# Attention accumulations of a decode kernel with gradients: four cache blocks per matmul, 512 wide

## The chip, the cores and the metric

The kernel runs on one core of a Trainium2 chip. Time is device time in microseconds (us), from the first to the last instruction as the chip reports it. The kernel before the change takes 1138.2 us, the median of three runs (1136.74 to 1139.24).

## The reference

Two identical decoder layers, one token for each of two sequences, forward and backward. A layer is grouped attention over a long cache and then a small MLP; both layers use the same caches and the same weights. Cut to what matters here:

```python
B, Sq, D = 2, 1, 1024
Hq, Hkv, Sk, Dh = 32, 4, 16384, 128          # 8 query heads share one cache head

def _A_ref(x, k_cache, v_cache, wq, wo):
    q = (x @ wq).reshape(B, Sq, Hq, Dh).transpose(0, 2, 1, 3)
    k, v = repeat(k_cache, 8, axis=1), repeat(v_cache, 8, axis=1)
    scores = einsum("bhqd,bhkd->bhqk", q, k) * (Dh ** -0.5)
    p = softmax(scores)
    o = einsum("bhqk,bhkd->bhqd", p, v)
    return o.transpose(0, 2, 1, 3).reshape(B, Sq, Hq * Dh) @ wo

x = x + _A_ref(_layernorm(x), k_cache, v_cache, wq, wo)     # layer 0
x = x + _B_ref(_layernorm(x), w1, b1, w2, b2)
x = x + _A_ref(_layernorm(x), k_cache, v_cache, wq, wo)     # layer 1
x = x + _B_ref(_layernorm(x), w1, b1, w2, b2)
# returned: x and the gradients of all inputs, for a given grad_out
```

There are 2 x 4 = 8 groups g (a sequence and a cache head), each with a K and a V cache of 16384 x 128 in bf16, 4 MB. Four sums over a whole cache concern us: the forward output o = sum of p x V in layer 0 and in layer 1, and in the backward pass of each layer dq = sum of ds x K, where ds is the gradient of the scores.

## The kernel before

A cache of 16384 rows is kept as 128 partitions x 128 blocks: partition p holds rows 128p to 128p + 127, and "block t" is row t of every partition, a matrix of 128 x 128. The kernel reads a cache in four chunks of 32 blocks, 1 MB each, into a ring of seven buffers. The exponentials of both layers stay in e_all, for group, pair of blocks u, layer l, head h and block t within the pair:

```python
TC = 32; NCH = T // TC; CP = TC // 2; NP = T // 2       # T = 128 blocks
e_all = pers.tile([128, G, NP, 2, 8, 2], BF16, name="e_all")
ACCT = pa([128, 512], F32, "acc_all")                   # one PSUM bank
```

One call of `quad` adds 16 blocks to an accumulator. The stationary operand of a matmul is the 16 columns of coefficients of one pair (8 heads x 2 blocks), the moving operand is two blocks of the cache side by side, 256 wide. Four of these matmuls go to four groups of 32 columns of the array (and 32 partitions of the accumulator), and four more follow. Of each 16 x 256 result only the parts where the block of the coefficient is that of the cache are wanted; sel2 picks these, and adds the four partition groups and the two blocks, in `reduce`:

```python
sel2 = const.tile([128, 16], F32, name="sel2")          # four 16-wide pieces of the identity, added
sel2v = sel2[:].rearrange("p (h t) -> p t h", t=2)

class Acc:
    def __init__(self, g, src, coef, finish, half=0):
        self.acc = ACCT[:, half * 256:half * 256 + 256] if half < 2 else pm_([128, 256], F32, "acc2")[:]
        zero = lambda: V.memset(self.acc, 0.0)
        ...

    def quad(self, c, q, coef=None):
        ...
        for i in range(8):
            u = c * CP + q * 8 + i
            cg = 32 * (i % 4)
            t = 2 * (q * 8 + i)
            PE.matmul(self.acc[cg:cg + 16, :], lhsT=coef(u),
                      rhs=self.cv[:, t:t + 2, :].rearrange("p t d -> p (t d)"),
                      start=False, stop=True, tile_position=(0, cg), skip_group_check=True)      # L452

    def evac(self):
        self.sb = wrk.tile([128, 2, 128], F32, name="acc_sb")
        evac_cast(self.sb[:].rearrange("p a b -> p (a b)"), self.acc, 256)
        ...

    def reduce(self):
        ps = px([128, 8], F32, "o_ps")[:] if self.alloc is None else self.alloc()[:, 0:8]
        for t in range(2):
            PE.matmul(ps, lhsT=self.sb[:, t, :], rhs=sel2v[:, t, :], start=(t == 0), stop=(t == 1))
        self.finish(ps)
```

Two accumulators share the bank ACCT, for alternating groups. The forward pass works in slots of eight blocks: eight transposes of K blocks (L420), a copy to SBUF by ScalarE or VectorE, and two slots later eight matmuls with the queries (L573). When a group's scores are complete, 16 exponentials follow, and its eight quads on V are taken from a queue, one in two slots, while the next group's scores are made:

```python
a = Acc(g, "V", lambda u: e_all[:, g, u, l].rearrange("p h t -> p (h t)"), finish, g % 2)
...
sch.later(9, lambda: queue_acc(sch, a, range(0, 2), False))
sch.later(13, lambda: queue_acc(sch, a, range(2, 4), True))
```

The layer-1 backward pass has the same slots with V transposed (L420) and the output's gradient in place of the queries (L672). After each chunk one product on VectorE makes ds, and two quads on K follow. Two chunks' ds lie interleaved in one buffer:

```python
dXr = [wrk.tile([128, CP, 2, 8, 2], BF16, name="dX%d" % i)[:] for i in range(3)]
...
ds = dXr[k // 2 % 3][:, :, k % 2]
ev = e_all[:, g, c * CP:(c + 1) * CP, l, :, :].rearrange("p a h b -> p h a b")
V.tensor_tensor(out=ds.rearrange("p a h b -> p h a b"),
                in0=dp[:].rearrange("p h (a b) -> p h a b", b=2), in1=ev, op=ALU.mult)            # L642
...
coef = lambda u: ds[:, u - c * CP].rearrange("p h t -> p (h t)")
```

The last pass is the backward of layer 0. It also makes the gradients of both caches for both layers (L1260: four matmuls 512 wide on halves of the rows, each evacuated by a copy and stored) and those of the weights (L1174), and does layer 0's dq on the way. dX holds the ds of both layers there:

```python
accs[g].coef = lambda u: dX[i][:, u - c * CP, 0].rearrange("p h t -> p (h t)")
```

Of the kernel before, what the change touches and what calls it, by code (L numbers as in the profile page):

```python
# [10 lines left out]
F32 = mybir.dt.float32  # L11
I32 = mybir.dt.int32
ACT = mybir.ActivationFunctionType
ALU = mybir.AluOpType
# [9 lines left out]
def kernel(  # L24
# [24 lines left out]
    nc = tc.nc  # L49
# [65 lines left out]
    V.memset(ones_bf[:], 1.0)  # L115
    neghalf = const.tile([128, 2], F32, name="neghalf")
    V.memset(neghalf[:], -0.5)
    sel2 = const.tile([128, 16], F32, name="sel2")
    V.tensor_tensor(out=sel2[:], in0=identf[:, 0:16], in1=identf[:, 32:48], op=ALU.add)
    V.tensor_tensor(out=sel2[:], in0=sel2[:], in1=identf[:, 64:80], op=ALU.add)  # L120
    V.tensor_tensor(out=sel2[:], in0=sel2[:], in1=identf[:, 96:112], op=ALU.add)
    sel2v = sel2[:].rearrange("p (h t) -> p t h", t=2)
    e_all = pers.tile([128, G, NP, 2, 8, 2], BF16, name="e_all")
    hot3 = const.tile([128, 128], BF16, name="hot3")
    m3 = const.tile([128, 1], F32, name="m3")
    V.tensor_reduce(out=m3[:], in_=identf[:, 64:128:32], axis=AX.X, op=ALU.add)
# [298 lines left out]
    class Acc:  # L425

        def __init__(self, g, src, coef, finish, half=0):
            self.g, self.src, self.coef, self.finish = g, src, coef, finish  # L430
            self.pre = {}
            self.cv = None
            self.acc = ACCT[:, half * 256:half * 256 + 256] if half < 2 else pm_([128, 256], F32, "acc2")[:]
            self.half = half
            zero = lambda: V.memset(self.acc, 0.0)
            if half in Acc.in_use:
                Acc.then[half] = zero
            else:
                zero()
            Acc.in_use.add(half)  # L440

        def quad(self, c, q, coef=None):
            coef = coef or self.coef
            if q == 0 and self.get is not None:
                self.cv = self.get(c)
            elif q == 0:
                self.cv = self.pre.pop(c) if c in self.pre else kv_load(self.src, self.g, c)
            for i in range(8):
                u = c * CP + q * 8 + i
                cg = 32 * (i % 4)  # L450
                t = 2 * (q * 8 + i)
                PE.matmul(self.acc[cg:cg + 16, :], lhsT=coef(u),  # L452
                          rhs=self.cv[:, t:t + 2, :].rearrange("p t d -> p (t d)"),
                          start=False, stop=True, tile_position=(0, cg), skip_group_check=True)

        def evac(self):
            self.sb = wrk.tile([128, 2, 128], F32, name="acc_sb")
            evac_cast(self.sb[:].rearrange("p a b -> p (a b)"), self.acc, 256)
            if self.half in Acc.then:
                Acc.then.pop(self.half)()  # L460
            else:
                Acc.in_use.remove(self.half)

        def reduce(self):
            ps = px([128, 8], F32, "o_ps")[:] if self.alloc is None else self.alloc()[:, 0:8]
            for t in range(2):
                PE.matmul(ps, lhsT=self.sb[:, t, :], rhs=sel2v[:, t, :], start=(t == 0), stop=(t == 1))
            self.finish(ps)

        alloc = get = None  # L470
# [30 lines left out]
    def attn_fwd(l, q_bf, rbc, oT, groups):  # L501
        sch = Sched()
        slots = [(g, c, b) for g in groups for c in range(NCH) for b in range(NB)]
        kTs, sc, st = {}, {}, {}

        def max_half(g, f):
            m = small.tile([128, 8], F32, name="mx%d" % f)
            V.tensor_reduce(out=m[:], in_=sc[g][f][:], axis=AX.X, op=ALU.max)
            charge("D", 0.7)
            st[g].append(m)  # L510

        def post(g):
            max_half(g, 1)
            m0, m1 = st[g]
            V.tensor_tensor(out=m0[:], in0=m0[:], in1=m1[:], op=ALU.max)
            esum = small.tile([128, 2, 8], F32, name="esum")
            negm = small.tile([128, 8], F32, name="negm")
            box = {}

            def p1():  # L520
                box["pm"] = pm_([8, 128], F32, "pm")
                PE.transpose(box["pm"][:, :], m0[:], identf[:])
                gm = small.tile([8, 1], F32, name="gm")
                V.reduce_max(out=gm[:], in_=box["pm"][:, :], axis=AX.X)
                box["dg"] = small.tile([8, 8], F32, name="dg")
                V.tensor_scalar(out=box["dg"][:], in0=identf[0:8, 0:8], scalar1=gm[:, 0:1], scalar2=None, op0=ALU.mult)
                charge("D", 0.5)

            def p2():
                pm2 = pm_([128, 8], F32, "pm2")  # L530
                PE.matmul(pm2[:], lhsT=onesf[0:8, :], rhs=box["dg"][:], start=True, stop=True)
                V.tensor_scalar(out=negm[:], in0=pm2[:], scalar1=-1.0, scalar2=None, op0=ALU.mult)  # L532
                charge("D", 0.2)

            def ex(f, h):
                half = NP // 2
                S.activation(out=e_all[:, g, f * half:(f + 1) * half, l, h, :],  # L537
                             in_=sc[g][f][:, h, :].rearrange("p (a b) -> p a b", b=2),
                             func=ACT.Exp, bias=negm[:, h:h + 1], scale=1.0, accum_out=esum[:, f, h:h + 1])
                charge("A", 0.3)  # L540

            def fin1():
                V.tensor_tensor(out=esum[:, 0, :], in0=esum[:, 0, :], in1=esum[:, 1, :], op=ALU.add)

            def fin2():
                pm3 = part_sum(esum[:, 0, :], 8, "pm3")
                V.reciprocal(out=rbc[:, g, :], in_=pm3[:])

            def finish(ps):
                V.tensor_tensor(out=oT[:, g, :], in0=ps, in1=rbc[:, g, :], op=ALU.mult)  # L550

            a = Acc(g, "V", lambda u: e_all[:, g, u, l].rearrange("p h t -> p (h t)"), finish, g % 2)
            sch.later(2, p1)
            sch.later(4, p2)
            for i in range(16):
                sch.later(5 + i // 2, lambda i=i: ex(i // 8, i % 8))
            sch.later(9, lambda: queue_acc(sch, a, range(0, 2), False))
            sch.later(13, lambda: queue_acc(sch, a, range(2, 4), True))
            sch.later(14, fin1)
            sch.later(15, fin2)  # L560

        def score(s):
            g, c, b = slots[s]
            if c == 0 and b == 0:
                sc[g] = {}
                st[g] = []
            kT = kTs.pop(s)
            for j in range(8):
                t = c * TC + b * 8 + j
                f = t // TH  # L570
                if t % TH == 0:
                    sc[g][f] = px([128, 8, TH], F32, "sc")
                PE.matmul(sc[g][f][:, :, t % TH], lhsT=kT[:, j, :], rhs=q_bf[:, g, :], start=True, stop=True)  # L573
            if c == NCH // 2 - 1 and b == NB - 1:
                max_half(g, 0)
            if c == NCH - 1 and b == NB - 1:
                post(g)

        cv = None
        s = 0  # L580
        while s < len(slots) + 2 or sch.busy():
            sch.s = s
            if s < len(slots):
                g, c, b = slots[s]
                if b == 0:
                    cv = kv_load("K", g, c)
                kTs[s] = emit_T(cv, b, True)
            sch.run_slot(1 if s < len(slots) else 2)
            if 2 <= s < len(slots) + 2:
                score(s - 2)  # L590
            s += 1

    def attn_bwd(l, do_bf, dqT, dn, groups, ahead):
# [40 lines left out]
        def post(g, c):  # L634
# [2 lines left out]
                      rhs=dlr[:, g, l, :].unsqueeze(2).to_broadcast([128, 8, TC]), start=False, stop=True)  # L637
            k = made["n"]
            made["n"] += 1
            ds = dXr[k // 2 % 3][:, :, k % 2]  # L640
            ev = e_all[:, g, c * CP:(c + 1) * CP, l, :, :].rearrange("p a h b -> p h a b")
            V.tensor_tensor(out=ds.rearrange("p a h b -> p h a b"),  # L642
                            in0=dp[:].rearrange("p h (a b) -> p h a b", b=2), in1=ev, op=ALU.mult)
# [1 line left out]
            if c == 0:  # L645
                def finish(ps, g=g):
# [4 lines left out]
                        wq_n[g % HKV][3]()  # L651
                    elif done_g.count(g % HKV) == 2:
                        by_dots(g % HKV)
                accs[g] = Acc(g, "K", None, finish, 2 if g == G - 1 else groups.index(g) % 2)
            acc = accs[g]
            if g == groups[-1]:
                accs[g].pre[c] = kv_load("K", g, c)
                if c == NCH - 1:
                    for k in range(NLD - 2):
                        ahead.load(k)  # L660
                        j0, rb = ahead.chunks[k]
                        w2_q.extend(lambda j=j: ahead.row(j) for j in range(j0, j0 + rb))
            coef = lambda u: ds[:, u - c * CP].rearrange("p h t -> p (h t)")
            sch.later(2, lambda: queue_acc(sch, acc, [c], c == NCH - 1, coef))

        def score(s):
# [658 lines left out]
    def open_dq(g):  # L1325
        def finish(ps):
            V.tensor_scalar(out=dq0[:, g, :], in0=ps, scalar1=QSCALE, scalar2=None, op0=ALU.mult)
            ready.append(g)
            if len(ready) % 2 == 0:
                quarter(g % HKV)  # L1330
        accs[g] = Acc(g, "K", None, finish, order.index(g) % 2)
        accs[g].alloc = mx
        accs[g].get = lambda c: (held_tiles["K%d" % c] if g == G - 1 else get("K", g, c))[:].rearrange(
            "p (t d) -> p t d", d=128)

    def dq_quad(i, q):
        g, c = chunks[i]
        accs[g].coef = lambda u: dX[i][:, u - c * CP, 0].rearrange("p h t -> p (h t)")
        accs[g].quad(c, q)
        if q == 1:  # L1340
            if g == G - 1:
# [202 lines left out]
```

## Time and profile before

| stage | from, us | to, us | quads in it |
|---|---|---|---|
| query projection, layer 0 | 0 | 28 | - |
| attention forward, layer 0 | 28 | 185 | 64 |
| output projection, MLP, projection of layer 1 | 185 | 271 | - |
| attention forward, layer 1 | 271 | 422 | 64 |
| MLP of layer 1, forward and backward, output projection backward | 422 | 502 | - |
| attention backward, layer 1 | 502 | 660 | 64 |
| MLP backward, layer 0, and what leads to the last pass | 660 | 737 | - |
| last pass: attention backward of layer 0, all cache and weight gradients | 737 | 1136 | 64 |

How to read the lines of the profile that follow below: PE is TensorE's matmul, PEld its weight load, DVE is VectorE, ACT ScalarE, POOL GpSimd, SP the engine that issues loads. "L452" is line 452 of the kernel. A group's line has engine, operation, output and inputs by the program's names, the active rows and columns of the array (128*16), the shape, and the count; then busy time in us and the mean duration of one in ns; then how long the engine was idle ahead of these instructions, and what it waited for. Matmuls are pipelined, so that busy time is the time covered by at least one, and the mean duration is longer than the time between two starts. In the 40 slices a digit is a share in tenths, 9 for 90% or more; PEclk is the granted share of TensorE's full clock.

The profiled execution took 1136.1 us from the first to the last instruction, with a mean granted clock of 0.882, and read 348.14 MB and wrote 98.58 MB of device memory.

### The profile page before, as it was taken

To read this page: it belongs to the slowest core of one execution; us is meant where nothing else is said; L and a number is where in the kernel's file an instruction comes from. 1 tells how busy PE (TensorE), PEld (TensorE's weight loads), DVE (VectorE), ACT (ScalarE), POOL (GpSimd) and SP (SyncE) were. 2 spreads that over 40 slices of the span, in tenths; PEclk is the share of its full clock that TensorE was granted. 3 is DMA by queue.
4 is the path that set the end of the run, shared out by engine and by line. 5 is a ranking of instruction groups with operands and counts; after the bars stand their busy time and mean duration, and the time that the engine had idled before them with its cause. 6 is when DMAs were issued, how large, how long until landed. Compare 5 with 4: busy or idle time off the path is not lost.

```text
span 1136.1 us, 38923 instructions
## 1 busy us (share of the span) xinstructions
PE 945.3 (83%) x17087; PEld 715.0 (63%) x17087; DVE 637.6 (56%) x1391; ACT 567.5 (50%) x1414; POOL 70.1 (6%) x124
## 2 busy tenths in 40 slices
PE   4978796487879885899998699988898897898896
PEld 3867675487767665898876588855555454455452
DVE  1545442133545432444746454778788767787776
ACT  0544342022535340344554344767787756686674
POOL 0000000000000000000000000022111111111210
PEclk9988976596998976899998899999999978898987
DMA  9999999998999989999999999998999999999997
GB/s 371 424 424 424 424 425 412 405 379 354 423 426 424 423 320 422 392 350 393 380 422 418 359 371 336 364 367 311 394 418 423 423 419 423 424 412 421 422 402 288
DMA packets 91962, 449.24 MB, mean 395 GB/s; under 512 B 7302, under 2 KB 7302, under 8 KB 54672
## 3 DMA queue, kind: packets, MB, share of 16 engines
q1 hardware_dynamic: 74448, 354.46, 77.4%
q0 software_dynamic: 17344, 92.29, 19.7%
q8 instruction: 133, 2.18, 0.7%
q14 instruction: 37, 0.30, 0.1%
HBM read 348.14 MB, written 98.58 MB: 393 GB/s over the span
## 4 chain that ended last, share of the span: by engine, by line
PE 50%; DMA 31%; DVE 10%; issue 4%; ACT 3%; POOL 0%; DVEq 0%; POOLq 0%; ACTq 0%; SPq 0%
DMA kv_V<-in_A_v_cache_dram 13%; PE tp L420 10%; PE wtp L270 5%; DMA kv_K<-in_A_k_cache_dram 5%; PE tpm L1451 4%; PE acc_all L452 4%; PE xm L1260 4%; DMA wt<-in_A_wo_dram 3%; DMA out_dram<-keepK 3%; DMA keepK<-in_A_v_cache_dram 3%; PE sc L573 3%; PE turn L322 3%; PE xm L1174 3%; PE dp L1313 2%; DMA out_dram<-keepxV 2%
## 5 line engine op out<-in xcount | busy, mean ns | idle before, releaser
L153 ACT COPY kT<-tp 128x512 int32<-128x512 int32 x209 | 122.8, 587 | 256.7 <-PE tp L420 247.9
L156 DVE COPY kT<-tp 128x1024 bf16<-128x1024 bf16 x159 | 108.8, 691 | 110.0 <-PE tp L420 99.1
L420 PE MATMUL tp<-ident,kv_K 128*128 128x128 bf16 x1728 | 140.3, 228 | 4.5 <-DMA kv_K<-in_A_k_cache_dram 4.5
L420 PEld LDWEIGHTS <-kv_K 128*128 128x128 bf16 x1728 | 106.3, 102 | 5.4 <-DMA kv_K<-in_A_k_cache_dram 5.3
L164 DVE CAST big<-xm 128x512 bf16<-128x512 f32 x133 | 86.4, 685 | 16.2 <-PE xm L1260 11.2
L161 ACT CAST big<-xm 128x512 bf16<-128x512 f32 x151 | 82.2, 595 | 23.2 <-PE xm L1260 13.0
L573 PEld LDWEIGHTS <-kT 128*128 128x128 bf16 x2048 | 75.9, 98 | 27.3 <-issue 21.0
L573 PE MATMUL sc<-qT_bf,kT 128*128 128x8 bf16 x2048 | 91.7, 171 | 0.3 <-issue 0.3
L161 ACT CAST keepV<-xm 128x512 bf16<-128x512 f32 (+1 forms) x137 | 75.1, 594 | 28.5 <-PE xm L1260 16.6
L420 PE MATMUL tp<-ident,kv_V 128*128 128x128 bf16 x864 | 71.5, 231 | 11.5 <-DMA kv_V<-in_A_v_cache_dram 10.6
L270 PE MATMUL wtp<-ident,wt 128*128 128x128 bf16 x928 | 75.9, 229 | 4.3 <-issue 2.9
L537 ACT ACTIVATE e_all<-sc,negm 128x64 bf16<-128x64 f32 x256 | 77.2, 345 | 1.1 <-DVE negm L532 1.0
L164 DVE CAST keepV<-xm 128x512 bf16<-128x512 f32 (+1 forms) x101 | 66.1, 685 | 18.6 <-PE xm L1260 12.3
L306 PEld LDWEIGHTS <-wt 128*128 128x128 bf16 x1696 | 48.8, 103 | 42.9 <-issue 15.2
L452 PE MATMUL acc_all<-kv_V,e_all 128*16 128x256 bf16 x864 | 46.2, 294 | 29.7 <-DMA kv_V<-in_A_v_cache_dram 16.7
L156 DVE COPY wT<-wtp 128x1024 bf16<-128x1024 bf16 (+1 forms) x64 | 41.1, 645 | 47.7 <-PE wtp L270 43.9
L153 ACT COPY wT<-wtp 128x512 int32<-128x512 int32 (+1 forms) x60 | 34.1, 568 | 64.2 <-PE wtp L270 55.8
L420 PEld LDWEIGHTS <-kv_V 128*128 128x128 bf16 x864 | 56.7, 103 | 13.3 <-DMA kv_V<-in_A_v_cache_dram 11.3
L270 PEld LDWEIGHTS <-wt 128*128 128x128 bf16 x928 | 58.1, 102 | 5.0 <-issue 3.7
L537 ACT ACTIVATION_READ_ACCUMULATOR e_all<-sc,negm 128x1 f32 x256 | 60.1, 235 | 0.0
L161 ACT CAST keepK<-xm 128x512 bf16<-128x512 f32 x98 | 52.9, 596 | 13.5 <-PE xm L1260 7.6
L1313 PE MATMUL dp<-wdo,kT 128*128 128x64 bf16 x896 | 52.2, 205 | 0.0
(369 smaller groups left out, 1750.5 us busy)
## 6 DMA issues: line engine op xcount, KB each, us to landing
kv_K<-in_A_k_cache_dram SPq DMA_DIRECT2D x81, 1024.0 KB, 11.5
kv_V<-in_A_v_cache_dram SPq DMA_DIRECT2D x81, 1024.0 KB, 12.5
wt<-in_A_wo_dram SPq DMA_DIRECT2D x32, 1024.0 KB, 9.9
wt<-in_B_w_dram SPq DMA_DIRECT2D x32, 896.0 KB, 14.0
out_dram<-big POOLq DMA_DIRECT2D x26, 1024.0 KB, 19.0
out_dram<-keepV POOLq DMA_DIRECT2D x19, 1024.0 KB, 20.0
out_dram<-keepK POOLq DMA_DIRECT2D x17, 1024.0 KB, 17.8
wt<-in_A_wq_dram SPq DMA_DIRECT2D x16, 1024.0 KB, 9.0
```

The lines of the kernel that those rows point to most:

```text
L153: S.copy(out=dst.bitcast(I32), in_=src.bitcast(I32))
L156: V.tensor_copy(out=dst, in_=src)
L161: S.copy(out=dst, in_=src)
L164: V.tensor_copy(out=dst, in_=src)
L270: PE.transpose(tp[:, o, :], wv[:, j, (o0 + o) * 128:(o0 + o + 1) * 128], ident[:])
L306: PE.matmul(fps[:, jo, :].rearrange("p (a b) -> p a b", b=2), lhsT=wv[:, j, jo * 128:(jo + 1) * 128], rhs=xT_bf[:, j0 + j, :].unsqueeze(1) ...
L420: PE.transpose(tp[:, j, :], cv[:, b * 8 + j, :], ident[:])
L452: PE.matmul(self.acc[cg:cg + 16, :], lhsT=coef(u), rhs=self.cv[:, t:t + 2, :].rearrange("p t d -> p (t d)"), start=False, stop=True, tile_ ...
L537: S.activation(out=e_all[:, g, f * half:(f + 1) * half, l, h, :], in_=sc[g][f][:, h, :].rearrange("p (a b) -> p a b", b=2), func=ACT.Exp, ...
L573: PE.matmul(sc[g][f][:, :, t % TH], lhsT=kT[:, j, :], rhs=q_bf[:, g, :], start=True, stop=True)
L1260: PE.matmul(pss[k][:], lhsT=blk[p:p + 64, o + 2 * h + k // 2, :], rhs=Qm[p:p + 64, :, :].rearrange("p a b -> p (a b)"), start=True, stop=T ...
L1313: PE.matmul(dp[:, :, t:t + 4], lhsT=kT[:, j, :], rhs=wd[:, :, x:x + 4], start=(b + j == 0), stop=False)
```

## The change

The stationary operand of one accumulation matmul becomes the coefficients of two pairs, and the moving operand four blocks, 512 wide. A quad is then four matmuls in place of eight. In the forward passes and in the last pass the coefficients of two pairs with both layers' columns are 64 adjacent columns of e_all (or of dX), so both layers' are loaded, and the other layer's results are not used; in layer 0 the other layer's part of e_all is not yet computed, so it is set to zero at the start. In the layer-1 backward pass ds is laid out by chunk, so that two pairs are 32 adjacent columns. Accumulators now lie on different halves of the partitions of the bank ACCT (rows 0 to 63 and 64 to 127) and take all its 512 columns. `evac` copies the two wanted diagonal parts, each 256 wide, and `reduce` uses 64 partitions with a selection matrix for its layer. The aim is half as many accumulation matmuls and weight loads, each of the greatest width.

```diff
-    sel2 = const.tile([128, 16], F32, name="sel2")
-    V.tensor_tensor(out=sel2[:], in0=identf[:, 0:16], in1=identf[:, 32:48], op=ALU.add)
 ...
+    sel_l = const.tile([128, 32], F32, name="sel_l")
+    V.tensor_tensor(out=sel_l[:], in0=identf[:, 0:32], in1=identf[:, 32:64], op=ALU.add)
 ... (two more for sel_l, three for sel_u)
     e_all = pers.tile([128, G, NP, 2, 8, 2], BF16, name="e_all")
+    nc.gpsimd.memset(e_all[:, :, :, 1].rearrange("p g u h t -> p (g u) (h t)").bitcast(I32), 0)
 ...
-            self.acc = ACCT[:, half * 256:half * 256 + 256] if half < 2 else pm_([128, 256], F32, "acc2")[:]
+            self.r = 64 * (half % 2)
+            bank = ACCT if half < 2 else pm_([128, 512], F32, "acc2")
+            self.acc = bank[self.r:self.r + (64 if l < 2 else 32), :]
             zero = lambda: V.memset(self.acc, 0.0)
 ...
-            for i in range(8):
-                u = c * CP + q * 8 + i
-                cg = 32 * (i % 4)
-                t = 2 * (q * 8 + i)
-                PE.matmul(self.acc[cg:cg + 16, :], lhsT=coef(u),
-                          rhs=self.cv[:, t:t + 2, :].rearrange("p t d -> p (t d)"),
-                          start=False, stop=True, tile_position=(0, cg), skip_group_check=True)
+            for t in range(16 * q, 16 * q + 16, 4):
+                PE.matmul(self.acc, lhsT=coef(c * CP + t // 2), rhs=self.cv[:, t:t + 4, :].rearrange("p t d -> p (t d)"),
+                          start=False, stop=True, tile_position=(0, self.r), skip_group_check=True)
 
         def evac(self):
             self.sb = wrk.tile([128, 2, 128], F32, name="acc_sb")
-            evac_cast(self.sb[:].rearrange("p a b -> p (a b)"), self.acc, 256)
+            for k in range(2):
+                src = self.acc[32 * k:32 * k + 32] if self.l < 2 else self.acc
+                evac_cast(self.sb[self.r + 32 * k:self.r + 32 * k + 32].rearrange("p a b -> p (a b)"),
+                          src[:, 256 * k:256 * k + 256], 256)
 ...
+            p = slice(self.r, self.r + 64)
             for t in range(2):
-                PE.matmul(ps, lhsT=self.sb[:, t, :], rhs=sel2v[:, t, :], start=(t == 0), stop=(t == 1))
+                PE.matmul(ps, lhsT=self.sb[p, t, :], rhs=sels[self.l][p, t, :], start=(t == 0), stop=(t == 1),
+                          tile_position=(self.r, 0))
 ...
-            a = Acc(g, "V", lambda u: e_all[:, g, u, l].rearrange("p h t -> p (h t)"), finish, g % 2)
+            a = Acc(g, "V", lambda u: e_all[:, g, u:u + 2].rearrange("p u l h t -> p (u l h t)"), finish, g % 2, l)
 ...
-            ds = dXr[k // 2 % 3][:, :, k % 2]
+            ds = dXr[k // 2 % 3].rearrange("p a l h b -> p (a l h b)")[:, k % 2 * 256:k % 2 * 256 + 256]
+            ds = ds.rearrange("p (a h b) -> p a h b", h=8, b=2)
 ...
-                accs[g] = Acc(g, "K", None, finish, 2 if g == G - 1 else groups.index(g) % 2)
+                accs[g] = Acc(g, "K", None, finish, 2 if g == G - 1 else groups.index(g) % 2, 2)
 ...
-            coef = lambda u: ds[:, u - c * CP].rearrange("p h t -> p (h t)")
+            coef = lambda u: ds[:, u - c * CP:u - c * CP + 2].rearrange("p u h t -> p (u h t)")
 ...
-        accs[g] = Acc(g, "K", None, finish, order.index(g) % 2)
+        accs[g] = Acc(g, "K", None, finish, order.index(g) % 2, 0)
 ...
-        accs[g].coef = lambda u: dX[i][:, u - c * CP, 0].rearrange("p h t -> p (h t)")
+        accs[g].coef = lambda u: dX[i][:, u - c * CP:u - c * CP + 2].rearrange("p u l h t -> p (u l h t)")
```

More of the change, by code (lines that the diff above doesn't have):

```diff
@@ L117 @@
     V.memset(neghalf[:], -0.5)
-    sel2 = const.tile([128, 16], F32, name="sel2")
-    V.tensor_tensor(out=sel2[:], in0=identf[:, 0:16], in1=identf[:, 32:48], op=ALU.add)
-    V.tensor_tensor(out=sel2[:], in0=sel2[:], in1=identf[:, 64:80], op=ALU.add)
-    V.tensor_tensor(out=sel2[:], in0=sel2[:], in1=identf[:, 96:112], op=ALU.add)
-    sel2v = sel2[:].rearrange("p (h t) -> p t h", t=2)
+    sel_l = const.tile([128, 32], F32, name="sel_l")
+    V.tensor_tensor(out=sel_l[:], in0=identf[:, 0:32], in1=identf[:, 32:64], op=ALU.add)
+    V.tensor_tensor(out=sel_l[:], in0=sel_l[:], in1=identf[:, 64:96], op=ALU.add)
+    V.tensor_tensor(out=sel_l[:], in0=sel_l[:], in1=identf[:, 96:128], op=ALU.add)
+    sels = [sel_l[:, 16 * l:16 * l + 16].rearrange("p (h t) -> p t h", t=2) for l in range(2)]
+    sel_u = const.tile([128, 16], F32, name="sel_u")
+    V.tensor_tensor(out=sel_u[:], in0=identf[:, 0:16], in1=identf[:, 48:64], op=ALU.add)
+    V.tensor_tensor(out=sel_u[:], in0=sel_u[:], in1=identf[:, 64:80], op=ALU.add)
+    V.tensor_tensor(out=sel_u[:], in0=sel_u[:], in1=identf[:, 112:128], op=ALU.add)
+    sels.append(sel_u[:].rearrange("p (h t) -> p t h", t=2))
     e_all = pers.tile([128, G, NP, 2, 8, 2], BF16, name="e_all")
+    nc.gpsimd.memset(e_all[:, :, :, 1].rearrange("p g u h t -> p (g u) (h t)").bitcast(I32), 0)
     hot3 = const.tile([128, 128], BF16, name="hot3")
@@ L425, with __init__ @@
     class Acc:
-        def __init__(self, g, src, coef, finish, half=0):
-            self.g, self.src, self.coef, self.finish = g, src, coef, finish
+        def __init__(self, g, src, coef, finish, half=0, l=0):
+            self.g, self.src, self.coef, self.finish, self.half, self.l = g, src, coef, finish, half, l
             self.pre = {}
             self.cv = None
-            self.acc = ACCT[:, half * 256:half * 256 + 256] if half < 2 else pm_([128, 256], F32, "acc2")[:]
-            self.half = half
+            self.r = 64 * (half % 2)
+            bank = ACCT if half < 2 else pm_([128, 512], F32, "acc2")
+            self.acc = bank[self.r:self.r + (64 if l < 2 else 32), :]
             zero = lambda: V.memset(self.acc, 0.0)
```

## Prediction

> **What bounds the kernel now.** First the top of the page: the engines' busy times and the span in 40 slices.
>
> ```profile
> PE 945.3 (83%) x17087; PEld 715.0 (63%) x17087; DVE 637.6 (56%) x1391; ACT 567.5 (50%) x1414; POOL 70.1 (6%) x124
> ...
> PE   4978796487879885899998699988898897898896
> ...
> PEclk9988976596998976899998899999999978898987
> DMA  9999999998999989999999999998999999999997
> ```
>
> The DMA engines are busy nine tenths or more almost everywhere, and TensorE comes next. 83% is a mean over stages, so I cut the span at the stages' ends. The columns are length, busy time (and instructions) of PE, PEld, DVE, ACT and POOL, granted TensorE clock, DMA share, GB/s.
>
> ```profile
> 28.00:185.00 157.00, 133.16 (x2594) 109.79 (x2591) 71.85 (x154) 70.30 (x311) 0.00 (x0) 0.88 1.01 424
> 271.00:422.00 151.00, 131.22 (x2632) 108.02 (x2633) 72.36 (x161) 71.10 (x313) 0.00 (x0) 0.91 1.00 415
> 502.00:580.00 78.00, 75.67 (x1635) 63.20 (x1636) 45.77 (x98) 36.06 (x64) 0.00 (x0) 0.98 0.96 382
> 580.00:660.00 80.00, 62.17 (x1169) 50.86 (x1168) 37.60 (x87) 37.23 (x68) 0.00 (x0) 0.87 0.98 390
> 737.00:850.00 113.00, 100.33 (x1434) 61.75 (x1433) 90.25 (x173) 85.20 (x163) 21.33 (x38) 0.98 0.96 371
> 850.00:1060.00 210.00, 185.25 (x2106) 102.92 (x2103) 161.93 (x297) 150.56 (x286) 34.10 (x55) 0.87 1.02 421
> 1060.00:1136.00 76.00, 58.82 (x620) 30.82 (x619) 52.51 (x101) 46.14 (x87) 7.36 (x13) 0.85 0.89 365
> ```
>
> The two forward passes (28 to 185, 271 to 422) are bound by DMA: share 1.0 at 415 to 424 GB/s, with TensorE 85 to 87% busy. The first half of the layer-1 backward pass (502 to 580) is bound by TensorE: 75.7 of 78 us. The last pass is bound by TensorE with both copying engines close behind until 850, and by DMA from there to 1060. In no stage is TensorE far from its limit.
>
> Then the matmuls that are to change, and a neighbour that has the new width. First the group of the forward accumulation, then pieces of TensorE's timeline in the layer-1 backward pass and in the last pass (start, length, what), then two lines of the table of waits (total, times, longest).
>
> ```profile
> L452 PE MATMUL acc_all<-kv_V,e_all 128*16 128x256 bf16 x864 | 46.2, 294 | 29.7 <-DMA kv_V<-in_A_v_cache_dram 16.7
> ```
>
> ```profile
> 520.26 0.40 PE L452 MATMUL acc_all<-kv_K,dX 128*16 128x256 bf16 x8
> 520.58 0.36 PE L672 MATMUL dp<-doT_bf,kT 128*128 128x8 bf16 x8
> 520.80 0.61 PE L420 MATMUL tp<-ident,kv_V 128*128 128x128 bf16 x8
> 521.24 0.35 PE L672 MATMUL dp<-doT_bf,kT 128*128 128x8 bf16 x8
> ...
> 871.01 0.61 PE L1260 MATMUL xm<-QmV,blk 64*128 64x512 bf16 x4
> ```
>
> ```profile
> SPq L409 <- PE acc_all L452: 148.3, 60, 6.0
> ...
> PE acc_all L452 <- DVE acc_all L435: 12.5, 15, 1.3
> ```
>
> One accumulation matmul takes 294 ns on average, but 864 of them occupy only 46.2 us, 53 ns each. The timeline says why. Eight transposes of 128 columns start at 520.80 and the next group starts at 521.24: 0.44 us, 55 ns per 128 columns. Eight matmuls of 256 columns in single file would need 8 x 110 = 880 ns; they begin at 520.26 and the next group begins at 520.58, 0.32 us later. Instruction by instruction the trace has four starting within 10 ns of each other, one in each group of 32 columns, and the other four 113 ns later. So a "quad" (one call of the accumulation, 16 cache blocks) is two rounds of about 110 ns plus some 100 ns before the next group begins. The four matmuls of line 1260 use the two halves of the rows in turn; one lasts 386 ns and all four 610, so the second pair begins 610 - 386 = 0.22 us after the first. That is what a 512-wide matmul holds its part of the array.
>
> **What the Trainium skill says.** "TensorEngine Tiling (Array Packing)", section Key Properties: tiles run weight loads and matmuls independently, and a change of tiling mode drains the engine. This agrees: four starts in 10 ns, and the 0.1 us after a quad. The same page, When to Use Tiling: up to 32 stationary columns allow four column tiles at once, up to 64 allow two. The old code fills all four; the new code sends all its matmuls to one tile. "TensorE: Matmul & The Clock Gate", Back-to-back issue gap: an isolated 512-wide matmul spaces starts by about 216 ns, and a sustained stream is given as 131 ns. The 0.22 us of line 1260 agrees with the first figure; I take that. The same page's Part 1: an array that idles falls to half clock, and sustained work lifts it. The mean clock of 0.87 to 0.91 in the stages with idle time and 0.98 in the full ones agrees.
>
> **The change, part by part.**
> *Removed:* 4 of 8 accumulation matmuls and weight loads per quad. The passes have 8 groups x 4 chunks x 2 quads = 64 quads each, four passes, 256 quads. 1024 matmuls fewer of 17087. Their issue was not the limit: starts 3 ns apart.
> *Added on TensorE:* the columns streamed per quad stay 2048 (8 x 256 = 4 x 512), but the new matmuls all have the tile position (0, r) with one r for the whole accumulator. They cannot run beside each other. A quad becomes 4 x 0.22 = 0.88 us plus the same 0.10: 0.98 instead of 0.32. I round the difference to 0.65 us at full clock. This is 64 x 0.65 = 42 us per pass and 166 us in all. The wider stationary operand (64 or 32 columns for 16) loads beside the previous matmul, as the second round's loads already do, and costs nothing.
> *Added on the copying engines:* each of 32 accumulators is evacuated in two copies in place of one. They have the same 256 columns on fewer partitions, so each takes the 0.37 to 0.42 us that acc_sb's copy takes now: 32 x 0.4 = 13 us over two engines that have room outside 737 to 850. The clearing memset goes from 256 to 512 columns: 272 to 485 ns by the width of the other memsets of this tile, 32 x 0.2 = 7 us. When TensorE waits for it now it loses 0.8 us, 12.5 us in all. The accumulators now lie on different partitions, which could end this wait or lengthen it; I put zero.
> *Start:* clearing half of e_all is 4096 words per partition on GpSimd. Its memset of 2048 elements took 1.82 us, so about 3.7 us, in a gap of 7.07 us before its first power. Three more small DVE additions, 0.6 us.
> *The layout of ds:* the product that writes it keeps its 0.42 us.
>
> **How much of the 42 us per pass lies on the path.** Room is the stage's length less PE busy. Part of today's busy time is at half clock and would shrink in a denser stage. With a mean clock of 0.88, 24% of the time is at half rate, and about half of the work done there would be saved. I allow for half of that gain, and then 5 to 8% of waits that a chain of transpose, copy and score doesn't lose.
> - Forward, layer 0: 133 + 42 = 175, less 8 for the clock, 167; with waits 172 against 157: +15.
> - Forward, layer 1: 131 + 42 = 173, less 6, 167; the last group's eight quads come after the scores with nothing beside half of them, some 3 us: 172 against 151: +21.
> - Layer-1 backward (158 us): 138 + 42 = 180, less 6, 174; with waits 180: +22.
> - Last pass. To 850 there are 23 quads, 15 us on a stage with 12.7 us of room and 80% busy copying engines: +9. To 1060 there are 31 quads, 20 us against 25 us of room under DMA: +3. After that 10 quads, 6.5 us: +4. Together +16.
> Sum: 15 + 21 + 22 + 16 = 74 us, under half of the 166. 1138 + 74 = 1212.
>
> **Rivals.**
> *Hidden under DMA.* With DMA share 1.0 in the forward passes, 42 us against 24 and 20 us of room is nearly hidden if the clock rises at once: two slots move 1.05 MB, 2.47 us at 424 GB/s, and TensorE's work for them is 2 x (0.44 + 0.22) + 0.98 + 0.1 = 2.4 us at full clock. Then forward gives +10 together, and the total is some +45: 1183. For it: the line of SPq, where loads wait 148 us in total for quads to give buffers back, so that transfers run to the limit of the buffers. Against it: that margin is 3% before small matmuls and waits, and no such margin exists at 502 to 580.
> *TensorE sets everything.* If the half clock stays and waits are not shared, each pass but the last loses the full excess, some 25 to 30 us, and the last 25: about +110, 1248.
> *Fewer instructions win.* If TensorE's cost were the number of instructions, 1024 pairs fewer would bring 1024 x 53 ns = 54 us less busy time, and some 20 us of span: 1118. Against it are the 3 ns starts. If the wait for the memset went too, it would be less still. I give this little.
>
> **Range and chances.** The rivals span 1118 to 1248. The concurrency of the old form and the single file of the new one are read straight from the timeline, so the sign is nearly sure; what is loose is how much DMA hides. Range 1172 to 1248. Faster by over 2% (below 1115) 0.03; within 2% (to 1161) 0.07; slower 0.90.
>
> **What would show it.** The accumulation should show 1024 matmuls of 512 columns and some 220 to 260 us busy, where line 452 has 104 in these stages now; a quad of four should hold TensorE for 0.9 us and more before the next group. PE should be at 95% or more from 28 to 185, 271 to 422 and 502 to 660, with DMA share below 0.95 there and a higher clock; 850 to 1060 should still be DMA-bound. I am wrong if the four matmuls start closer than 0.2 us to each other, if the forward stages keep their 157 and 151 us, or if waits for evacuation grow by more than some us.

## The result and the profile after

The changed kernel takes 1221.5 us (median of six runs, 1215.2 to 1226.5) against 1138.9 for the kernel before, measured beside it: ratio 1.072, 95% interval 1.068 to 1.076. For each experiment below the kernel before was measured again; its medians then are 1139.1 to 1139.2. The predicted time was 1212, in a range of 1172 to 1248.

The page's top and three rows of the slices, of the changed kernel:

```profile
PE 1062.1 (87%) x16063; PEld 741.8 (61%) x16063; DVE 653.1 (54%) x1410; ACT 575.1 (47%) x1430; POOL 73.8 (6%) x125
...
PE   4999898578989986899999889998989888898997
...
PEclk9999999597999987689999999999999999899988
DMA  9999998999999965999889999998899999999996
```

1024 matmuls fewer, and 117 us more of TensorE's time. The DMA row has holes where it had nines, and the clock row is fuller. The same stages as before, cut at the changed kernel's own stage ends (columns as before: length, PE, PEld, DVE, ACT, POOL, clock, DMA share, GB/s):

```profile
28.00:211.80 183.80, 165.90 (x2376) 119.07 (x2377) 75.81 (x166) 73.07 (x317) 0.00 (x0) 0.99 0.98 397
211.80:283.90 72.10, 49.70 (x1420) 48.16 (x1419) 19.17 (x57) 7.28 (x13) 2.07 (x3) 0.73 0.93 364
283.90:471.60 187.70, 168.79 (x2377) 120.21 (x2378) 75.69 (x165) 73.76 (x318) 0.00 (x0) 0.96 0.86 333
550.50:738.90 188.40, 175.50 (x2684) 124.27 (x2684) 89.58 (x208) 76.54 (x140) 0.00 (x0) 1.00 0.90 342
925.00:1140.00 215.00, 191.04 (x2054) 103.67 (x2052) 169.04 (x308) 156.82 (x297) 34.72 (x57) 0.97 1.02 421
```

The layer-1 forward pass moved from 415 to 333 GB/s: taken as a whole it is no longer bound by DMA, though its first 56 us still have a DMA share of 1.0. The layer-1 backward pass is at 342 GB/s. The layer-0 forward pass is near both limits: TensorE is busy for 90% of it, with a DMA share of 0.98, and some of that traffic is already for the next stage. The middle of the last pass still has DMA share 1.02. Then the accumulation's group, its place in the timeline of the layer-1 backward pass, and its waits:

```profile
L456 PE MATMUL acc_all<-kv_V,e_all 128*64 128x512 bf16 x432 | 115.4, 390 | 21.0 <-DVE acc_all L442 19.7
```

```profile
570.51 1.04 PE L456 MATMUL acc_all<-kv_K,dX 128*32 128x512 bf16 x4
571.48 0.36 PE L681 MATMUL dp<-doT_bf,kT 128*128 128x8 bf16 x8
```

```profile
PE acc_all L456 <- DVE acc_all L442: 21.9, 18, 1.6
```

Four matmuls begin at 570.51 and the next group at 571.48: 0.97 us a quad, where it was 0.32. The forward accumulation's 432 matmuls cover 115.4 us, 267 ns each; the old 864 covered 46.2. And the wait that stood first in the old group's line, for the V cache from DMA (16.7 us), is gone; the wait for the clearing memset has taken its place.

For the comparisons below each stage is taken from the first matmul of that stage in the trace to the first of the next (us). "Then" is the stage between two passes. A row is one execution, so that differences of 2 us or so are within its noise: the forward pass of layer 0 is the same code in one_tile_256 and in one_tile_forward0, and took 176.6 and 178.6.

| kernel | forward 0 | then | forward 1 | then | backward 1 | then | last pass |
|---|---|---|---|---|---|---|---|
| before | 162.9 | 80.7 | 151.4 | 79.5 | 164.3 | 66.3 | 403.3 |
| changed | 183.8 | 72.1 | 187.6 | 78.9 | 188.5 | 65.3 | 414.9 |
| one_tile_256 | 176.6 | 72.8 | 177.5 | 77.0 | 187.7 | 65.7 | 415.0 |
| two_tiles_256 | 163.1 | 80.3 | 154.7 | 77.5 | 169.7 | 66.2 | 406.4 |
| two_tiles_512 | 163.0 | 80.8 | 161.6 | 77.6 | 173.2 | 65.1 | 405.5 |
| after_no_memset | 174.3 | 72.5 | 175.5 | 77.9 | 187.0 | 65.8 | 414.6 |
| before_no_memset | 161.1 | 83.3 | 149.9 | 78.5 | 161.5 | 66.5 | 408.5 |
| one_tile_256_no_memset | 170.5 | 72.7 | 169.6 | 79.2 | 187.2 | 65.5 | 414.8 |
| full_bank_two_tiles | 166.6 | 76.8 | 162.6 | 79.5 | 172.0 | 65.0 | 412.2 |
| after_no_memset_one_copy | 170.9 | 73.6 | 169.1 | 77.5 | 186.8 | 65.5 | 415.6 |
| one_tile_forward0 | 178.6 | 72.4 | 152.6 | 78.5 | 162.7 | 66.1 | 404.6 |

The theory: matmuls on one column tile (one group of 32 or 64 columns of the array) run in single file. The first rival: the cost is in what came along (the width, the unused columns, two copies, a longer memset). Then it is to be found how much of the excess each stage hides.

### The profile page after: what moved, and what is told of

It is laid out like the page before. It is cut to its first block, busy times and chain, and to the rows that moved or that the text cites. A ratio compares the mean times of both kernels' runs of the same rounds, so it can differ in the third digit from the quotient of the medians.

```text
span 1219.1 us, 36915 instructions
## 1 busy us (share of the span) xinstructions
PE 1062.1 (87%) x16063; PEld 741.8 (61%) x16063; DVE 653.1 (54%) x1410; ACT 575.1 (47%) x1430; POOL 73.8 (6%) x125
## 4 chain that ended last, share of the span: by engine, by line
PE 70%; DVE 11%; DMA 10%; ACT 4%; issue 4%; POOL 0%; ACTq 0%; DVEq 0%; POOLq 0%; SPq 0%
PE acc_all L456 19%; PE tp L426 12%; PE wtp L276 5%; PE sc L581 4%; PE xm L1269 4%; PE tpm L1460 4%; PE xm L1183 3%; PE turn L328 2%; PE dp L1322 2%; PE dp L681 2%; DMA keepK<-in_A_v_cache_dram 2%; PE acc_all L312 2%; DMA kv_K<-in_A_k_cache_dram 2%; ACT e_all L545 2%; DMA out_dram<-keepxV 2%
## 5 line engine op out<-in xcount | busy, mean ns | idle before, releaser
L426 PE MATMUL tp<-ident,kv_K 128*128 128x128 bf16 x1728 | 134.6, 223 | 2.1 <-DMA kv_K<-in_A_k_cache_dram 2.1
L456 PE MATMUL acc_all<-kv_V,e_all 128*64 128x512 bf16 x432 | 115.4, 390 | 21.0 <-DVE acc_all L442 19.7
L426 PEld LDWEIGHTS <-kv_K 128*128 128x128 bf16 x1728 | 101.8, 99 | 2.2 <-DMA kv_K<-in_A_k_cache_dram 2.2
L167 ACT CAST big<-xm 128x512 bf16<-128x512 f32 x157 | 84.3, 593 | 25.1 <-PE xm L1183 14.1
L167 ACT CAST keepV<-xm 128x512 bf16<-128x512 f32 (+1 forms) x134 | 72.6, 590 | 40.2 <-PE xm L1269 22.3
L170 DVE CAST big<-xm 128x512 bf16<-128x512 f32 x127 | 82.5, 684 | 16.8 <-PE xm L1269 9.6
L456 PEld LDWEIGHTS <-e_all 128*64 128x64 bf16 x512 | 49.2, 112 | 66.8 <-issue 25.3
L456 PEld LDWEIGHTS <-dX 128*32 128x32 bf16 (+1 forms) x480 | 40.4, 102 | 49.6 <-issue 12.9
L426 PE MATMUL tp<-ident,kv_V 128*128 128x128 bf16 x864 | 65.3, 218 | 4.5 <-DMA kv_V<-in_A_v_cache_dram 3.3
L456 PE MATMUL acc_all<-kv_K,dX 128*32 128x512 bf16 x216 | 55.6, 381 | 2.5 <-DVE acc_all L442 2.0
## 6 DMA issues: line engine op xcount, KB each, us to landing
wt<-in_B_w_dram SPq DMA_DIRECT2D x32, 896.0 KB, 12.5
```

The costliest lines, as they stand in the source:

```text
L167: S.copy(out=dst, in_=src)
L170: V.tensor_copy(out=dst, in_=src)
L426: PE.transpose(tp[:, j, :], cv[:, b * 8 + j, :], ident[:])
L456: PE.matmul(self.acc, lhsT=coef(c * CP + t // 2), rhs=self.cv[:, t:t + 4, :].rearrange("p t d -> p (t d)"), start=False, stop=True, tile_p ...
```

## Experiments

### one_tile_256: single file alone

```diff
-                cg = 32 * (i % 4)
+                cg = 0
```
(in the kernel before)

> The kernel before with one edit: all eight 256-wide matmuls of a quad go to the column tile at 0. Nothing of the change itself is in it: 16 stationary columns, one evacuation, the old layout of ds. Theory (matmuls of one tile run in single file): a quad holds TensorE for 8 x 0.11 + 0.1 = 0.98 us in place of 0.32, as in the changed kernel, and the time is 1205 to 1222. Rival (the cost is the width, the unused columns, or the doubled evacuation and memset): 1138 to 1150.

Measured: 1203.9 us, ratio 1.057 (1.054 to 1.060). This kernel has nothing of the change but its single file, and has 65 of its 83 us of loss. In its timeline of the forward pass a quad holds TensorE for 62.98 - 62.00 = 0.98 us:

```profile
62.00 1.04 PE L452 MATMUL acc_all<-kv_V,e_all 128*16 128x256 bf16 x8
62.98 0.36 PE L573 MATMUL sc<-qT_bf,kT 128*128 128x8 bf16 x8
```

A rival would be that the eight matmuls wait for each other because they add to the same accumulator. The traces speak against it: in the changed kernel four 512-wide matmuls on one accumulator start 216 ns apart (median), and the eight transposes beside them, each with a place of its own in PSUM, go at the same pace, 55 ns per 128 columns.

The remaining 17.5 us, to 1221.5, are for the other runs to explain. 1203.9 lies 1 us under the expected range.

### two_tiles_256: half of the tiles

```diff
-                cg = 32 * (i % 4)
+                cg = 32 * (i % 2)
```
(in the kernel before)

> The kernel before with two column tiles in use in place of four. Theory: four rounds, 4 x 0.11 + 0.1 = 0.54 us a quad, 0.22 us more than before, 14 us per pass; the forward passes have 20 to 24 us of room under DMA and hide most of it, the layer-1 backward pass does not: 1148 to 1160, much less than a third of the loss of one tile. Rival (each step of serialization costs its share of TensorE time, nothing hidden): 1138 + 56 = 1194.

Measured: 1148.2 us, ratio 1.008 (1.006 to 1.010). The timeline has the 0.54 us that the theory gives:

```profile
60.40 0.61 PE L452 MATMUL acc_all<-kv_V,e_all 128*16 128x256 bf16 x8
60.93 0.36 PE L573 MATMUL sc<-qT_bf,kT 128*128 128x8 bf16 x8
```

256 x 0.22 = 56 us more of TensorE by this count, 9 us more of time: the forward pass of layer 0 keeps its length (163.1 for 162.9), and the layer-1 backward pass takes more than half of the loss. As long as TensorE's work doesn't fill a stage, most of the excess is hidden.

### two_tiles_512: the change's width on two tiles

```diff
-                PE.matmul(self.acc, lhsT=coef(c * CP + t // 2), ...
-                          ... tile_position=(0, self.r), ...)
+                j = 32 * (t // 4 % 2)
+                PE.matmul(self.acc[j:j + 32, :], lhsT=coef(c * CP + t // 2), ...
+                          ... tile_position=(0, self.r + j), ...)
...
-            a = Acc(g, "V", lambda u: e_all[:, g, u:u + 2]..., finish, g % 2, l)
+            a = Acc(g, "V", lambda u: e_all[:, g, u]..., finish, g % 2, l)      # 32 columns: one pair, both layers
...
-        accs[g].coef = lambda u: dX[i][:, u - c * CP:u - c * CP + 2]...
+        accs[g].coef = lambda u: dX[i][:, u - c * CP]...
```
(in the changed kernel)

> The changed kernel with its four 512-wide matmuls on two column tiles in turn (32 stationary columns each); two evacuation copies, the memset 512 wide and ds by chunk stay. In the forward passes and the last pass the 32 columns are those of one pair with both layers, not of two pairs, so the output is not the reference's; the work has the same size. Theory: 2 x 0.22 + 0.1 = 0.54 us a quad, and the time comes near that of two tiles at 256, up to 10 us above it for the longer memset and second copy: 1150 to 1168. Rival (width, copies or layout cost the time): above 1200.

Measured: 1152.6 us, ratio 1.012 (1.008 to 1.015). Memset, copies and layout are the changed kernel's, and 69 of its 83 us are gone. Even TensorE's waits for the memset are the changed kernel's, to the digit:

```profile
PE acc_all L457 <- DVE acc_all L442: 21.9, 18, 1.6
```

So these cost little by themselves as long as TensorE has room; single file makes them dear.

### after_no_memset: the wait that took DMA's place

```diff
-            zero = lambda: V.memset(self.acc, 0.0)
-            ... (and its call when an accumulator is free)
+            self.first = True
...
-                          start=False, stop=True, tile_position=(0, self.r), ...)
+                          start=self.first, stop=True, tile_position=(0, self.r), ...)
+                self.first = False
```
(in the changed kernel)

> The changed kernel without the clearing of accumulators: the first matmul of each overwrites in place of adding (possible because the two accumulators lie on different partitions now). Theory: TensorE's waits for the memset, 21.9 us in the changed kernel, were hidden under DMA before and lie on the path now; without them 1200 to 1210, and 8 to 10 us of it in the layer-1 forward pass. Rival (the wait is only moved, to the evacuation of the accumulator before): 1218 to 1224.

Measured: 1198.9 us, ratio 1.053 (1.050 to 1.056), 22.6 us less than the changed kernel and a little more gain than expected; 9.5 and 12.1 us of it are in the two forward passes. The wait is not moved: TensorE's waits for the evacuation copies stay at 7.2 us. How it came about is seen in the changed kernel's timeline of all engines:

```profile
60.37 0.48 DVE L442 MEMSET acc_all<- 64x512 f32 x1 [0.16 <-issue]
60.91 1.02 PE L456 MATMUL acc_all<-kv_V,e_all 128*64 128x512 bf16 x4 [1.17 <-DVE acc_all L442]
```

By the program's order this memset clears the accumulator of the next group, whose first quad comes some nine slots later; the quad that waits belongs to the group before it, on the other half of the partitions of the same bank. It stands still 1.17 us for a memset of 0.48 that comes behind VectorE's maximum over the scores. Fourteen of the 18 waits are of this kind, seven in each forward pass: one for every group after the first.

### before_no_memset: the same edit where DMA sets the pace

```diff
-                          start=False, stop=True, tile_position=(0, cg), ...)
+                          start=self.n < 4, stop=True, tile_position=(0, cg), ...)
+                self.n += 1
```
(in the kernel before, with its memset taken out likewise, but for one of the third accumulator)

> The kernel before (eight 256-wide matmuls on four column tiles) without the clearing of accumulators: the first matmul in each column tile overwrites. TensorE waits 12.5 us for this memset in the kernel before. Theory: the forward passes, where most of the waits are, are bound by DMA there, so little of it is on the path: 1130 to 1138, a gain of at most 8 us, against 22.6 us that the same edit brought in the changed kernel. Rival (the wait costs the same wherever it stands): 1125 or less.

Measured: 1136.0 us, ratio 0.998 (0.996 to 0.999). The same edit brings 3.3 us here by the medians and 22.6 us in the changed kernel. This is the only version that is faster than both kernels, and by little. Its waits say where the time of the memset goes when it is taken away (this execution took 1138.7 us, 2.8 over the median):

```profile
PE acc_all L449 <- DMA kv_V<-in_A_v_cache_dram: 25.1, 16, 2.8
```

The wait for the V cache grows from 16.7 to 25.1 us: TensorE, let go by the memset, waits for DMA. In the table the forward pass of layer 0 is 1.8 us shorter and the stage after it 2.6 longer.

### one_tile_256_no_memset: what width is worth

Both edits on the kernel before: `cg = 0`, and no memset (but for the third accumulator's); sel2 takes the first 16 partitions alone.

> As the run before, but all eight matmuls on one column tile. Set against the changed kernel without memset (1198.9), it leaves the width, the wider stationary operand, the second evacuation copy and the layout of ds as the only differences. Theory (columns in single file are the cost, and the width of a matmul is worth nothing either way): 1192 to 1203. Rival (512 wide saves issue or weight loads): above 1205. Rival (the second copy and the wider loads cost time): below 1190.

Measured: 1187.4 us, ratio 1.043 (1.041 to 1.044): 11.4 us below the changed kernel without memset. The theory's interval is missed and the second rival's holds: with single file the same, the 512-wide form is not equal but worse. Over the whole quads of the traces the time from the first matmul to the next group has a median of 973 ns here; in the changed kernel without memset it is 983 ns where the stationary operand has 64 columns (three of the four passes) and 970 where it has 32. 10 ns x 192 = 1.9 us. The rest has to be elsewhere.

Set against one_tile_256 (1203.9), this run also gives the cleanest price of the memset. Its length is that of the kernel before (0.27 us), and only the pace of TensorE differs. TensorE's waits for it in one_tile_256 are hardly more than the 12.5 us of the kernel before:

```profile
PE acc_all L452 <- DVE acc_all L435: 14.7, 16, 1.3
```

Taking it out brings 16.5 us here, and 3.3 in the kernel before.

### after_no_memset_one_copy: the second copy

```diff
+            if self.l < 2:
+                evac_cast(self.sb[self.r:self.r + 64]..., self.acc[:, 0:256], 256)
-            for k in range(2):
+            for k in range(2 if self.l == 2 else 0):
```
(in the changed kernel without memset; the sums of odd pairs are left out)

> The changed kernel without memset, and in the forward passes and the last pass one evacuation copy of 64 partitions by 256 columns in place of two of 32 partitions. It leaves out the sums of the odd pairs, so the output is not the reference's; the layer-1 backward pass keeps its two copies. Against the kernel before on one tile without memset (1187.4) the changed kernel without memset (1198.9) is 11.5 us slower. Theory (the two copies read one bank one after the other, and the reduction on TensorE waits for both: 12 us of such waits in its trace against 3): 1188 to 1193, with the gain in the two forward passes. Rival (the wider weight loads, 10 ns a quad, and the rest of the width): 1196 to 1200.

Measured: 1189.6 us, ratio 1.046 (1.043 to 1.049). By the medians the second copy costs 9.3 of the 11.4 us, and 3.4 and 6.4 us of gain lie in the two forward passes. The six times spread from 1188.5 to 1198.4, so that the 9.3 is good to 4 or 5 us. TensorE's waits for the copy ahead of the reduction, in the changed kernel without memset:

```profile
PE o_ps L466 <- DVE acc_sb L170: 4.5, 7, 1.0
PE o_ps L466 <- ACT acc_sb L167: 2.7, 5, 0.8
```

and with one copy:

```profile
PE o_ps L468 <- DVE acc_sb L170: 1.0, 2, 0.5
PE o_ps L468 <- ACT acc_sb L167: 0.8, 1, 0.8
```

These waits shrink by 5.4 us, so they account for over half of the 9.3; where the rest lies is not shown. The copying engines had room; TensorE, next in line, had none.

### full_bank_two_tiles: the change's own columns on two tiles

```diff
-            self.acc = bank[self.r:self.r + (64 if l < 2 else 32), :]
+            self.acc = bank
...
+                r = 64 * (self.n % 2)
+                PE.matmul(self.acc[r:r + self.m, :], ..., start=self.n < 2, ..., tile_position=(0, r), ...)
...
-            for k in range(2):
+            for r in (0, 64):
+                for k in range(2):
```
(in the changed kernel, without memset; m is 64 or 32)

> The changed kernel's operands (64 columns, 512 wide, ds by chunk), but a quad's four matmuls alternate between partitions 0 to 63 and 64 to 127, so an accumulator takes the whole bank, with four evacuation copies and no memset; a group's first quad has to wait for the evacuation of the one before. Theory: a quad takes 2 x 0.22 + 0.1 = 0.54 us, and the time is that of two tiles at 256 (1148) less a few us for the memset and plus some for the waits on evacuation: 1140 to 1155. Rival (the waits on evacuation, some 1 us for each of 32 groups, all count): 1170 to 1180.

Measured: 1162.6 us, ratio 1.022 (1.020 to 1.024). It missed: between the two expectations. Quads take 555 ns with 64 columns, as they should. But the four copies wait for each other (34.2 us in all), and TensorE for the copies, in its table of waits:

```profile
PE o_ps L468 <- ACT acc_sb L167: 7.9, 7, 1.7
PE o_ps L468 <- DVE acc_sb L170: 7.7, 7, 1.9
```

With the change's own operands it is 59 us faster than the changed kernel, and 36 us faster than that without memset, which is the like comparison. It stays 14 us behind two tiles at 256; the waits for the evacuation are the likely reason, but no run takes them away.

### one_tile_forward0: what a stage gives back

```diff
-                cg = 32 * (i % 4)
+                cg = 0 if self.one else 32 * (i % 4)       # one: layer 0's forward pass
```
(in the kernel before)

> The kernel before with one column tile in the forward pass of layer 0 alone. With one tile everywhere that pass took 13.7 us longer and the stage after it 7.9 us less. Theory (loads of the next stage's weights go ahead while TensorE sets the pace, so part of the loss is given back at once): net +4 to +8, 1143 to 1147. Rival (the give-back has another cause and the whole loss stays): +13 to +15, 1152 to 1154.

Measured: 1145.6 us, ratio 1.006 (1.005 to 1.007), 6.4 us more. The forward pass takes 15.7 us longer and the stage after it 8.3 us less. In every kernel whose first pass is longer by 3 us or more, that stage is shorter, between 72.1 and 76.8 for 80.7. TensorE's timeline at its start, first of the kernel before, then of the changed one:

```profile
192.96 1.03 PE L306 MATMUL acc_all<-o_all,wt 128*128 128x32 bf16 x32 [0.43 <-DMA wt<-in_A_wo_dram]
195.52 1.03 PE L306 MATMUL acc_all<-o_all,wt 128*128 128x32 bf16 x32 [1.53 <-DMA wt<-in_A_wo_dram]
```

```profile
211.80 5.82 PE L312 MATMUL acc_all<-o_all,wt 128*128 128x32 bf16 x218 [0.88 <-DVE acc_all L301]
```

Before, each 1 MB of weights is waited for, 1.5 us apiece. After, most of them lie in the ring of buffers already, loaded while TensorE was still on its quads, and 218 matmuls run in one piece.

## Why the prediction was right, point by point

In sign and in its main mechanism, the single file, it was right, and the measured time is 9 us above the predicted one. But the runs show that this nearness is in part luck: too large a share of the excess was put on the path, while the memset and the second copy were left out, and these errors cancel. Walking from the kernel before to the changed one by runs (medians): 1139.2, without memset 1136.0; one tile 1187.4 (+51.5); 512 wide with one copy 1189.6 (+2.2), with two 1198.9 (+9.3); with the memset 1221.5 (+22.6).

- *The cost of a quad, 0.32 to 0.98 us.* Right: 0.97 in the changed kernel's timeline, 0.98 with eight 256-wide matmuls on one tile. The column tiles ran beside each other as the Trainium skill has it ("TensorEngine Tiling (Array Packing)", section Key Properties), and one, two and four of them give medians of 973, 539 and 328 ns (one_tile_256, two_tiles_256, before). The sustained 131 ns for a 512-wide matmul, from the Trainium skill's "TensorE: Matmul & The Clock Gate", section Back-to-back issue gap, does not hold on one tile: the starts are 216 ns apart, and four take 0.97 us.
- *Fewer instructions are worth nothing.* Right: with one copy and no memset the wide form was not faster. The 2.2 us by which it was slower lie within the spread of its runs.
- *How much of the 166 us is on the path.* Predicted 74, measured 51.5 with the memset out on both sides, and 64.9 with the old memset in (one_tile_256 against before); the difference is what the memset itself comes to cost.
- *Stage by stage, by the pair without memset.* The forward pass of layer 0 has +9.4 for a predicted +15, and 10.6 us given back in the next stage: nothing left. The prediction looked at each stage's own room under DMA, and not at loads that run ahead across its end. After the forward pass of layer 1 there is nothing to give back: even in the kernel before, TensorE waits there only 0.6 us for the first weights, against 8.1 in layer 0, as the last group's caches are in SBUF already and loads run ahead. So the pass has +19.7 for a predicted +21. The layer-1 backward pass has +25.7 for +22. The last pass has +6.3 (+11.6 in the changed kernel against before) for +16, and its middle stayed bound by DMA, as predicted. The largest miss in the changed kernel itself is the forward pass of layer 1, +36.2 for +21; 12.1 of it went with the memset and 6.4 with the second copy.
- *The memset: "I put zero".* This is the step that failed. It costs 22.6 us in the changed kernel; the 5 us of general waits that the prediction allowed in the forward pass of layer 0 don't cover the 9.5 us that went with it there. The trace of before had its 12.5 us of waits, but they stood where DMA had 16.7 us of waits of its own, and cost 3.3. Once TensorE sets the pace they are on the path: 14.7 us of waits cost 16.5 with the old memset, and in the changed kernel, whose memset takes 0.48 us in place of 0.27, 21.9 us of waits cost 22.6. That accumulators lie on different partitions did not end the wait, as the waiting quads of the other half show.
- *The second copy: on engines with room.* Wrong too: some 9 us. The prediction asked whether VectorE and ScalarE had time for 13 us, and not who waits for the copy.
- *The tail of a forward pass.* Predicted 3 us. In layer 1 the last group's quads take from 415.50 to the evacuation at 420.44 before, and from 460.02 to 469.11 after: 4.2 us more.
- *Clock.* As expected it rose with the work, from 0.88 to 0.945 over the span, and to 0.99 and 1.00 in the first forward and the layer-1 backward pass.
- *The signs that it named.* The four matmuls start 216 ns apart and no closer than 0.2 us, and both forward passes grew: so far no sign of being wrong. The third sign came: TensorE's waits for evacuation grew from 1.6 to 7.2 us, and that was the second copy. The forecast of 95% and more of PE did not hold in the changed kernel (90, 90 and 93% in the two forward passes and the layer-1 backward pass), nor a DMA share below 0.95 in the first of them (0.98). Without the memset the changed kernel has 95% in both forward passes: its waits are what was missing there.
- *The start.* First transposes at 27.8 us before and 28.0 after: the clearing of e_all cost nothing there.

The rival "hidden under DMA" (1183) comes near the truth for the forward pass of layer 0 alone, and there because of loads that run ahead across its end. "TensorE sets everything" (1248) was too much: the middle of the last pass stayed under DMA, and the clock rose. "Fewer instructions" (1118) fell.

## What to carry to other kernels

A matmul with few stationary columns should be counted by rounds, not by columns streamed: small products on different column tiles run beside each other, and merging them into fewer, wider ones on one tile can lose that factor (here a quad went from 0.33 to 0.98 us). When a change makes another engine the bound of a stage, go through the waits of that engine in the old trace which cost nothing so far (here a memset and a copy) and put them on the path. The memset's waits went there in full. And look past a stage's end: what the bound engine loses there may come back at once where the next stage had been waiting for the other one.

## What was not expected of the hardware

A quad on one tile takes 973 ns with 16 stationary columns and eight 256-wide matmuls, 970 with 32 and four 512-wide ones, 983 with 64: on one tile it is nearly the columns streamed alone that count, and four times the stationary columns add 1%. An evacuation copy of 32 partitions by 256 takes 0.36 us on ScalarE and 0.42 on VectorE, as one of 128 partitions does (0.38 and 0.42): with the same 256 columns fewer partitions saved no time here, and an evacuation cut in two by partitions was twice the work.
